# Off-by-one attention and slotted soft MoE: one exponential for both heads of a pair, on a hand-numbered ring of PSUM banks

## The chip, the cores and the metric

The kernel runs on one core of one Trainium2 chip (trn2). The metric is the time of one execution in microseconds on the device. Five engines with queues of their own take part: TensorE (PE; its weight loads are shown as PEld), VectorE (DVE), ScalarE (ACT), GpSimd (POOL), which also issues most of the DMAs, and SyncE (SP), which issues the others. The sums of TensorE stand in PSUM, in eight banks of 2 KB for each of 128 partitions.

## The reference

```python
# q, k, v: (8, 12, 448, 64)
scores = scale * np.matmul(q, k.transpose(0, 1, 3, 2))
m = np.max(scores, axis=-1, keepdims=True)
e = np.exp(scores - m)
attn = e / (np.sum(e, axis=-1, keepdims=True) + np.exp(-m) + 1e-09)
x = np.matmul(attn, v)                 # heads side by side: (3584, 768)

logits = x @ phi                       # phi: (768, 32), 8 experts of 4 slots
d = softmax of logits over the 3584 tokens
slot_input = d.T @ x                   # (32, 768)
for e in range(8):                     # on the 4 slots of expert e
    slot_out[e] = np.maximum(slot_input[e] @ w1[e], 0) @ w2[e]    # 768 -> 1024 -> 768
c = softmax of logits over the 32 slots
out = c @ slot_out                     # (3584, 768), float32
```

The first softmax has one more term, exp(-m), in its denominator. Maxima and exponentials of the scores are what the change is about.

## The kernel before

**Work.** The 96 pairs of batch and head are taken two heads at a time: NPAIR = 48 pairs, six (PB) to a batch, three (NP) to a group of loads. The two heads of a pair (hl = 0, 1) lie in the lower and upper 64 partitions. 448 tokens make three chunks of 128 and a half chunk of 64 (i = 3), in which both heads share the partitions. The program's order is kept as written on each engine (`manual_schedule`), so a queue waits when its next instruction waits.

**Slots.** The main loop has a slot s for each pair, with two halves y = 0 and 1. The parts of a slot:

- `T(n)`: 28 transposes of q and k of pair n (L262) into one bank, and one copy to SBUF, by ScalarE (L269) or VectorE (L271). In slot s it is pair s + 4.
- `A(n, i)`: the scores with queries on partitions (L290, or L307 for the half chunk) into a bank of `psA` (three banks) and their row maxima by VectorE (L291, L309). `runs` is the list of these, and each chunk of the loop takes the next one. They run one to two pairs ahead.
- `W2(n)`: turns the maxima of pair n (L316); VectorE copies them (mT, L318).
- `Bk(n, i)`: the scores with keys on partitions (L354, L383), from which `lower` takes the maximum by four more products (L337), and their exponentials by ScalarE (L358, L388). With `mix=True` the products of the next `A` are laced in: a0 of head 0, scores of head 1, scores of head 0, the four lowering products, the exponentials, a1 of head 1.
- `AV(n, i, qs)`: products of the exponentials with v and a column of ones (L422), into the one bank of `psV`; the ones give the denominators.
- `N1(n)`: copies that bank to `ubuf` (L435). `EC(g)`: exp(-m) of a group (L323). `N2(n)`: denominator by one VectorE instruction (L450), its reciprocal (L451), and by GpSimd three products that write x (L463), and two small instructions for the half chunk (L471, L472).
- `PX(n)`: turns x of pair n by four products (L493) into one bank, which ScalarE copies (L499). In slot s it is pair s - 2.
- `V(g)` (L394 to L397) and `slot_loads`: GpSimd's placing of v and its DMA issues, one group ahead. `P(b)` is the soft-MoE work of a batch (logits L527, their turn and maxima, exponentials, the sums of L615); its steps are spread over slots by `post`.

Before the change a slot goes so on TensorE: chunk 0, chunk 1 | twenty products of `AV`, W2 | chunk 2, half chunk, T, twelve products of `AV`, PX.

**Banks.** `psA` has three banks, `psV` one, and `psB` four that are taken in turn, one at a time, by the scores of `Bk` (two for a chunk, one for the half chunk), by T and by PX: nine takings a slot. A taking waits until the reader of the one four before is done.

After the loop the eight experts (L825, L845) and the output (L888) follow; they take the last 45 us or so, and the change leaves them as they are.

Of the kernel before, what the change touches and what calls it, by code (L numbers as in the profile page):

```python
# [24 lines left out]
HG = 6  # L25
NP = 3
# [5 lines left out]
def kernel(  # L32
# [123 lines left out]
    with ExitStack() as at:  # L156
# [9 lines left out]
        ubuf = pu.tile([128, 2, 7 * W65], F32, name="ubuf")  # L166
# [32 lines left out]
        def ones_in(t, eng):  # L199

            eng.memset(t, 0.0)
            eng.memset(t[:, :, 0:3, D:W65], 1.0)
            eng.memset(t[0:64, 0:HG:2, 3, D:W65], 1.0)
            eng.memset(t[64:128, 1:HG:2, 3, D:W65], 1.0)
# [3 lines left out]
        for hl in range(2):  # L208
            nc.vector.memset(halfm[64 - 64 * hl:128 - 64 * hl, hl:hl + 1], 1.0)
# [24 lines left out]
        def kcol(hl, tok):  # L234
            if hl == 0:
                return 384 if tok == 0 else (tok - 1) * 128 if tok < 4 else (tok - 4) * 128 + 64
            return tok * 128 if tok < 3 else (tok - 3) * 128 + 64 if tok < 6 else 384

        def qcol(hl, i):

            if i < 2:
                return slice(i * 128, i * 128 + 128)
            if i == 2:
                return slice(320, S) if hl == 0 else slice(256, 384)
            return slice(256, 320) if hl == 0 else slice(384, S)

        def T(n):
            g, pl = divmod(n, NP)
            first = n < 7
            ps = psB.tile([128, 2, S], BF16, tag="b", name="ps_t")  # L250

            k0 = [psB.tile([128, 2, S], BF16, tag="b", name="ps_k") for _ in range(2)] if n == 0 else None
# [11 lines left out]
            if n == 0:  # L264
                nc.scalar.copy(t[:, 0, :], ps[:, 0, :])
                nc.vector.tensor_copy(t[:, 1, 0:256], k0[0][:, 0, 0:256])
                nc.vector.tensor_copy(t[:, 1, 256:S], k0[1][:, 0, 256:S])
            elif first or n % 6 in (1, 3):
                nc.scalar.copy(t, ps)  # L269
            else:  # L270
                nc.vector.tensor_copy(t, ps)  # L271
            qkT[n] = t

        def mpos(i, hl=0):
            return 3 if i == 3 else i if hl else (5, 6, 4)[i]
# [5 lines left out]
        def A(n, i, steps=False):  # L283
# [18 lines left out]
            else:  # L302
                ps = psA.tile([128, 512], F32, tag="a", name="ps_a")

                for hl in range(2):
                    r = slice(64 * hl, 64 * hl + 64)
                    nc.tensor.matmul(ps[64 - 64 * hl:128 - 64 * hl, 0:S], t[r, 0, qcol(hl, 3)], t[r, 1, :],  # L307
# [12 lines left out]
        def EC(g):  # L320
            ec[g] = psm.tile([128, NP, 7], F32, tag="ec", name="ec", bufs=3)
            z = g % 2 * NP
            nc.scalar.activation(ec[g], mxr[:, z:z + NP, 0:7], AF.Exp, scale=-scale)  # L323
            if g == NG - 1:
                e, t = ec[g][:, NP - 1, :], psm.tile([128, 7], F32, name="ec_last", bufs=1)
                for o, i in ((slice(1, 6, 2), slice(0, 3)), (slice(0, 4, 2), slice(5, 7)), (slice(4, 5), slice(4, 5)),
                             (slice(6, 7), slice(3, 4))):
                    nc.gpsimd.tensor_copy(t[:, o], e[:, i])
                ec["last"] = t

        def lower(outs, n, m):

            for z in range(2):
                for hl, o in outs.items():
                    c = (5, 3) if hl == 0 else (0, 2)
                    src = slice(0, 256) if z == 0 else slice(64, 256) if hl == 0 else slice(0, 192)
                    nc.tensor.matmul(o[:, 256 * z:min(256 * z + 256, S)], sel[rs[hl], c[z]:c[z] + 1].to_broadcast([64, m]),  # L337
# [3 lines left out]
        def Bk(n, i, c=0, mix=False):  # L341

            t = qkT[n]
            if i < 3 and mix and runs and runs[0][1] < 3:
# [5 lines left out]
                pss = {}  # L350

                def score(hl):
                    pss[hl] = pb_("ps_b")
                    nc.tensor.matmul(pss[hl][:, 0:S], t[rs[hl], 1, cols], t[rs[hl], 0, :], start=True, stop=False,  # L354
                                     skip_group_check=True)

                def expo(hl):
                    nc.scalar.activation(e[:, hl, :], pss[hl][:, 0:S], AF.Exp, scale=scale)  # L358
                    eT[n, i, hl] = e[:, hl, :]
# [4 lines left out]
                lower({hl: pss[hl][:, 0:S] for hl in (1, 0)}, n, 128)  # L364
                expo(1)
                expo(0)
                a1()
                return
            if i < 3:
                pss = [pb_("ps_b") for _ in range(2)]  # L370
                outs = [p[:, 0:S] for p in pss]
# [4 lines left out]
            else:  # L376
                pss = [pb_("ps_b")]
                outs = [pss[0][r, 0:S] for r in rs]
# [8 lines left out]
            for p, e in zip(pss, es):  # L387
                nc.scalar.activation(e, p[:, 0:S], AF.Exp, scale=scale)  # L388
# [3 lines left out]
        def V(g):  # L392
            t, s = vp[g % 2], nat["v", g]
            nc.gpsimd.tensor_copy(t[:, 0:HG:2, 0:3, 0:D], s[:, 0:HG:2, 1:4, :])  # L394
            nc.gpsimd.tensor_copy(t[:, 1:HG:2, 0:3, 0:D], s[:, 1:HG:2, 0:3, :])
            nc.gpsimd.tensor_copy(t[0:64, 0:HG:2, 3, 0:D], s[0:64, 0:HG:2, 0, :])
            nc.gpsimd.tensor_copy(t[64:128, 1:HG:2, 3, 0:D], s[64:128, 1:HG:2, 3, :])  # L397
# [9 lines left out]
        def AV(n, i, qs):  # L407
# [6 lines left out]
            for u in qs:  # L414
                for hl in range(2):
                    if u < 3:
                        c0 = (2 * u + hl if n == NPAIR - 1 else mpos(u, hl)) * W65
                        o, qc = a[:, c0:c0 + W65], qcol(hl, u)
                    else:
                        t, z = (av_half["ps"], 0) if n == NPAIR - 1 else (a, 3 * W65)  # L420
                        o, qc = t[64 - 64 * hl:128 - 64 * hl, z:z + W65], qcol(hl, 3)
# [7 lines left out]
        def N1(n):  # L429
            src = av[n][:, 0:7 * W65].rearrange("p (s c) -> p s c", c=W65)  # L430
            if n == NPAIR - 1:
                us[n] = src
                return
            u = ubuf[:, n % 2, :].rearrange("p (s c) -> p s c", c=W65)
            (nc.scalar.copy if on_pool(n) else nc.vector.tensor_copy)(u, src)  # L435
            us[n] = u

        def N2(n):
            g, pl = divmod(n, NP)
            b, pb = divmod(n, PB)  # L440
            u = us[n]
            eng = nc.gpsimd if on_pool(n) else nc.vector
            rec = psm.tile([128, 7], F32, tag="rec", name="rec", bufs=3)
            e = ec[g][:, pl, :] if n < NPAIR - 1 else ec["last"]
            if n == NPAIR - 1:
                nc.vector.scalar_tensor_tensor(rec[:, 6:7], av_half["ps"][:, D:W65], 1e-9, e[:, 6:7],
                                               op0=ALU.add, op1=ALU.add)
                nc.vector.scalar_tensor_tensor(rec[:, 0:6], u[:, 0:6, D], 1e-9, e[:, 0:6], op0=ALU.add, op1=ALU.add)
            else:
# [5 lines left out]
            if n == NPAIR - 1:  # L455
                eng.tensor_mul(
                    x[:, 0:3, c:c + 128].rearrange("p i (h d) -> p i h d", h=2),
                    u[:, 0:6, 0:D].rearrange("p (i h) d -> p i h d", h=2),
                    rec[:, 0:6].rearrange("p (i h) -> p i h", h=2).unsqueeze(3).to_broadcast([128, 3, 2, D]))
            else:  # L460
# [4 lines left out]
            if n == NPAIR - 1:  # L465

                for h in range(2):
                    r = slice(64 - 64 * h, 128 - 64 * h)
                    nc.scalar.mul(x[r, 3, c + 64 * h:c + 64 * h + 64], av_half["ps"][r, 0:D], rec[r, 6:7])
                return  # L470
# [3 lines left out]
                u[:, 3, 0:D].unsqueeze(1).to_broadcast([128, 2, D]),  # L474
# [200 lines left out]
        runs = [(n, i) for n in range(NPAIR) for i in (0, 1, 3, 2)]  # L675
# [50 lines left out]
        for s in range(NPAIR + 1):  # L726
            for y in range(2):
                hs = 2 * s + y
                mix = len(runs) > 1 and runs[0][1] == 2 - y
                if mix:  # L730
                    Bk(s, 2 * y, mix=True)
                    Bk(s, 2 * y + 1, y, mix=True)
                else:
                    As(1)
                if mix:
                    pass
                elif s < NPAIR:
                    Bk(s, 2 * y)
                    side = int(y == 1 and len(runs) > 0 and runs[0][1] == 3)
                    Bk(s, 2 * y + 1, side)  # L740
                    As(1 - side)
                else:
                    As(1)
# [4 lines left out]
                else:  # L748
                    if s < NPAIR - 4:
                        T(s + 4 if s else 3)  # L750
                    if s < NPAIR:
                        for i in (0, 1):
                            AV(s, i, range(3))
# [241 lines left out]
```

## Time and profile before

| what | value |
|---|---|
| median of 3 runs | 304.77 us (303.82 to 565.14) |
| the profiled execution | 303.48 us, its span 301.4 us |
| mean granted TensorE clock | 0.952 |
| busy: PE, DVE, ACT, POOL | 274.6, 259.4, 245.1, 197.4 us |
| row maxima (L291, VectorE) | 276 of 613 ns |
| exponentials of a chunk (L358, ScalarE) | 276 of 566 ns |
| copies of turned q,k (L269 ScalarE; L271 VectorE) | 20 of 923 ns; 27 of 612 ns |
| copies of turned x (L499, ScalarE) | 47 of 607 ns |
| products for x (L463, GpSimd) | 135, of 505, 395 and 289 ns by size |

Busy times are unions: neighbouring instructions on an engine overlap a little, so the mean length of an instruction is more than its share of a full engine. The busy time of PE counts modelled ends of its pipelined products. In the answers shown below a line of instructions has the start in us from the start of the span, the time until the last of the group ends, engine, line, operation, what it writes and reads, and how many.

### The profile page before, as it was taken

What the parts mean: (1) busy time and instruction counts of PE and PEld (TensorE: products, weight loads), DVE (VectorE), ACT (ScalarE), POOL (GpSimd) and SP (SyncE); (2) the same over time, 40 slices, a digit from 0 to 9 for tenths busy, and PEclk for the clock granted to TensorE, in tenths of its full rate; (3) what the DMA queues carried; (4) which work ended last, traced back from release to release, by engine and by line L of the source; (5) the groups of instructions that cost most, each with busy time, mean ns of one, the idle gap of its engine ahead of it and who ended that gap; (6) DMA issues with size and microseconds to landing.
All of it is one profiled execution on the core that took longest, in us unless ns stands there. A gap on an engine that the chain in (4) does not pass through costs nothing.

```text
span 301.4 us, 13421 instructions
## 1 busy us (share of the span) xinstructions
PE 274.6 (91%) x5682; PEld 190.3 (63%) x5682; DVE 259.4 (86%) x626; ACT 245.1 (81%) x524; POOL 197.4 (65%) x433
## 2 busy tenths in 40 slices
PE   5899999999999999999999999999999999997820
PEld 3476767776766677767776777677767666662100
DVE  5989999999999999999999999999999996537840
ACT  3489999899889989998999899988998978337730
POOL 8767696878688959795979597959892763000000
PEclk9889999999999999999999999999999999998555
DMA  8999399999999999999999999999999699907997
GB/s 138 193 196 200 55 127 213 166 207 148 211 144 194 140 210 153 203 144 211 150 203 151 206 144 206 159 194 164 209 174 210 100 226 239 345 20 290 409 446 320
DMA packets 47275, 58.93 MB, mean 196 GB/s; under 512 B 2800, under 2 KB 40176, under 8 KB 46960
## 3 DMA queue, kind: packets, MB, share of 16 engines
q0 software_dynamic: 40432, 42.29, 87.8%
q1 hardware_dynamic: 6784, 15.80, 13.7%
q8 instruction: 44, 0.72, 0.9%
q14 instruction: 15, 0.12, 0.1%
HBM read 89.36 MB, written 15.34 MB: 347 GB/s over the span
## 4 chain that ended last, share of the span: by engine, by line
PE 58%; ACT 16%; DVE 16%; issue 5%; DMA 1%; DVEq 0%; ACTq 0%
PE ps_av L422 12%; PE ps_a L290 10%; DVE mxr L291 8%; PE ps_b L337 8%; PE ps_b L354 5%; ACT W L269 4%; PE ps_b L383 4%; PE ps_t L262 4%; ACT W L388 3%; ACT W L358 3%; ACT W L499 3%; PE ps_o L888 3%; PE ps_x L493 2%; PE ps_s L615 2%; PE ps_h L825 2%
## 5 line engine op out<-in xcount | busy, mean ns | idle before, releaser
L291 DVE TENSOR_REDUCE mxr<-ps_a 128x1 bf16<-128x448 f32 x276 | 153.7, 613 | 5.2 <-PE ps_a L290 5.0
L358 ACT ACTIVATE W<-ps_b 128x448 bf16<-128x448 f32 x276 | 131.8, 566 | 9.8 <-PE ps_a L290 5.4
L337 PE MATMUL ps_b<-mT,sel 64*128 64x192 bf16 (+3 forms) x768 | 94.3, 258 | 0.0
L290 PE MATMUL ps_a<-W 64*128 64x448 bf16 x276 | 90.2, 354 | 2.3 <-DVE mxr L291 1.9
L354 PE MATMUL ps_b<-W 64*128 64x448 bf16 x276 | 78.2, 354 | 2.6 <-ACT W L269 0.5
L463 POOL TENSOR_TENSOR W<-ubuf,rec 128x192 bf16<-128x192 f32 x135 | 50.0, 396 | 39.4 <-ACT W L499 25.3
L422 PE MATMUL ps_av<-W 128*128 128x65 bf16 (+1 forms) x1536 | 64.7, 196 | 0.6 <-issue 0.5
L422 PEld LDWEIGHTS <-W 128*128 128x128 bf16 (+1 forms) x1536 | 50.1, 100 | 21.5 <-issue 17.2
L337 PEld LDWEIGHTS <-sel 64*128 64x128 bf16 (+1 forms) x768 | 48.3, 98 | 22.5 <-issue 8.9
L499 ACT CAST W<-ps_x 128x512 bf16<-128x512 f32 x47 | 28.5, 607 | 10.8 <-PE ps_x L493 10.5
L388 ACT ACTIVATE W<-ps_b 128x448 bf16<-128x448 f32 x60 | 32.5, 562 | 1.6 <-PE ps_b L337 1.5
L290 PEld LDWEIGHTS <-W 64*128 64x128 bf16 x276 | 25.9, 94 | 11.6 <-issue 0.4
L262 PE MATMUL ps_t<-ident,W 64*64 64x64 bf16 x1330 | 29.8, 195 | 1.4 <-ACT W L213 1.4
L262 PEld LDWEIGHTS <-W 64*64 64x64 bf16 x1344 | 28.3, 112 | 3.6 <-issue 2.0
L309 DVE TENSOR_REDUCE mxr<-ps_a 128x1 bf16<-128x448 f32 x48 | 29.5, 615 | 0.1
L435 ACT COPY ubuf<-ps_av 128x455 f32<-128x455 f32 x45 | 26.1, 579 | 1.2 <-PE ps_av L422 0.6
L111 POOL DMA_DIRECT2D W<-in_moe_w_dram x30 | 22.6, 754 | 5.2 <-PE ps_b L337 4.2
L269 ACT COPY W<-ps_t 128x896 bf16<-128x896 bf16 x20 | 18.5, 923 | 3.8 <-PE ps_t L262 3.8
L383 PE MATMUL ps_b<-W 64*64 64x448 bf16 (+1 forms) x108 | 21.2, 375 | 0.1
L472 POOL TENSOR_TENSOR W<-ubuf,rec 128x128 bf16<-128x128 f32 x45 | 18.0, 400 | 3.7
L354 PEld LDWEIGHTS <-W 64*128 64x128 bf16 x276 | 18.2, 94 | 3.3 <-issue 1.9
L493 PE MATMUL ps_x<-ident,W 128*128 128x128 bf16 x192 | 18.7, 219 | 0.2
(146 smaller groups left out, 394.5 us busy)
## 6 DMA issues: line engine op xcount, KB each, us to landing
W<-in_moe_w_dram POOLq DMA_DIRECT2D x22, 768.0 KB, 9.6
W<-in_v_dram POOLq DMA_DIRECT2D x32, 192.0 KB, 4.9
out_dram<-W SPq DMA_DIRECT2D x2, 2688.0 KB, 9.3
W<-in_q_dram POOLq DMA_DIRECT2D x15, 336.0 KB, 4.9
W<-in_k_dram POOLq DMA_DIRECT2D x15, 336.0 KB, 6.6
stage<-in_moe_w_dram POOLq DMA_DIRECT2D x4, 768.0 KB, 10.1
W<-stage SPq DMA_DIRECT2D x5, 576.0 KB, 6.0
W<-in_moe_w_dram POOLq DMA_DIRECT2D x4, 576.0 KB, 8.1
```

The source lines that it names most:

```text
L262: nc.tensor.transpose(o, src[r, pl, tok * D:(tok + 1) * D], ident[r, r])
L269: nc.scalar.copy(t, ps)
L290: nc.tensor.matmul(ps[:, 0:S], t[r, 0, qcol(hl, i)], t[r, 1, :], start=True, stop=True)
L291: nc.vector.reduce_max(mcol(n, i, hl), ps[:, 0:S], axis=AX.X)
L337: nc.tensor.matmul(o[:, 256 * z:min(256 * z + 256, S)], sel[rs[hl], c[z]:c[z] + 1].to_broadcast([64, m]), mT[n][rs[hl], src], start=False, ...
L354: nc.tensor.matmul(pss[hl][:, 0:S], t[rs[hl], 1, cols], t[rs[hl], 0, :], start=True, stop=False, skip_group_check=True)
L358: nc.scalar.activation(e[:, hl, :], pss[hl][:, 0:S], AF.Exp, scale=scale)
L383: nc.tensor.matmul(outs[hl], t[rs[hl], 1, cols], t[rs[hl], 0, :], start=True, stop=False, skip_group_check=True)
L388: nc.scalar.activation(e, p[:, 0:S], AF.Exp, scale=scale)
L422: nc.tensor.matmul(o, eT[n, i, hl][:, qc], vp[g % 2][:, 2 * pl + hl, i, 0:W65], start=(i == 0 and u == 0 and hl == 0) or (u == 3 and i == ...
L463: eng.tensor_mul(x[:, i0:i1, c + 64 * h:c + 64 * h + 64], u[:, r, 0:D], rec[:, r].unsqueeze(2).to_broadcast([128, i1 - i0, D]))
L499: nc.scalar.copy(xT(b, pb), pss[0])
```

## The change

1. **Ring.** `psB` becomes one tile of four banks. `pb_(nm, n)` hands out the next bank, or for n = 2 the next two that begin at an even number; a bank left over is passed by.
2. **Exponentials.** Both heads of a chunk have their scores in two neighbouring banks, and one ScalarE instruction takes the exponentials of both (896 columns).
3. **Order.** In the second half of a slot the half chunk comes first, then T, then chunk 2; `runs` is in the order 0, 3, 1, 2. So a slot goes: chunk 0, chunk 1 | `AV`, W2 | half chunk, T, chunk 2, `AV`, PX.
4. **Turned copies.** From pair 7 on the copy of T goes to ScalarE for two pairs of three (before for one of three), and stands behind the exponential of chunk 2 (`late_copy`).
5. **Denominators.** `EC` adds 1e-9 on GpSimd; a new step `N1a` adds exp(-m) and the sums on GpSimd, behind N1 (in a group's last slot behind EC). VectorE keeps the reciprocal.
6. **x.** The two heads change places in the half chunk (`kcol`, `qcol`, `mpos`, `lower`, `V`), so that `ubuf` holds them as two rows of four and one GpSimd product of 3 x 2 x 64 writes what three wrote. The last pair needs no GpSimd copies of its exp(-m) any more.

```diff
-        psB = pool("psB", 4, space=PSUM)
+        psB = pool("psB", 1, space=PSUM)
-        pb_ = lambda nm: psB.tile([128, 512], F32, tag="b", name=nm)
+        ring = psB.tile([128, 4, 512], F32, name="ring")
+        at_bank = [0]
+        def pb_(nm="", n=1):
+            z = -(-at_bank[0] // n) * n % 4
+            at_bank[0] = (z + n) % 4
+            return ring[:, z, :] if n == 1 else ring[:, z:z + n, :]
+        pt_ = lambda: pb_().bitcast(BF16)[:, 0:2 * S].rearrange("p (a s) -> p a s", a=2)
...
         def T(n):
-            ps = psB.tile([128, 2, S], BF16, tag="b", name="ps_t")
+            ps = pt_()
...
-            elif first or n % 6 in (1, 3):
+            elif first:
                 nc.scalar.copy(t, ps)
+            elif n % 3 != 2:
+                late_copy.append((t, ps))
             else:
                 nc.vector.tensor_copy(t, ps)
...
         def EC(g):
-            ec[g] = psm.tile([128, NP, 7], F32, tag="ec", name="ec", bufs=3)
+            ec[g] = psm.tile([128, NP, 8], F32, tag="ec", name="ec", bufs=3)
-            nc.scalar.activation(ec[g], mxr[:, z:z + NP, 0:7], AF.Exp, scale=-scale)
-            if g == NG - 1:
...
+            nc.scalar.activation(ec[g][:, :, 0:7], mxr[:, z:z + NP, 0:7], AF.Exp, scale=-scale)
+            nc.gpsimd.tensor_scalar(ec[g][:, :, 0:7], ec[g][:, :, 0:7], 1e-9, None, op0=ALU.add)
...
         def Bk(n, i, c=0, mix=False):
...
-                    pss[hl] = pb_("ps_b")
+                ps = pb_("ps_b", 2)
...
-                expo(1)
-                expo(0)
+                nc.scalar.activation(e, ps[:, :, 0:S], AF.Exp, scale=scale)
+                for hl in range(2):
+                    eT[n, i, hl] = e[:, hl, :]
                 a1()
...
+        def N1a(n):
+            rec = psm.tile([128, 8], F32, tag="rec", name="rec", bufs=3)
+            u = ubuf[:, n % 2, :].rearrange("p (s c) -> p s c", c=W65)
+            nc.gpsimd.tensor_add(rec[:, 0:7], u[:, 0:7, D], ec[n // NP][:, n % NP, 0:7])
+            us[n] = rec
...
         def N2(n):
-                nc.vector.scalar_tensor_tensor(rec, u[:, :, D], 1e-9, e, op0=ALU.add, op1=ALU.add)
-            nc.vector.reciprocal(rec, rec)
-                for i0, i1, z, h in ((0, 3, 0, 1), (0, 2, 5, 0), (2, 3, 4, 0)):
-                    r = slice(z, z + i1 - i0)
-                    eng.tensor_mul(x[:, i0:i1, c + 64 * h:c + 64 * h + 64], u[:, r, 0:D],
-                                   rec[:, r].unsqueeze(2).to_broadcast([128, i1 - i0, D]))
+            rec, eng = us[n], nc.gpsimd if on_pool(n) else nc.vector
+            nc.vector.reciprocal(rec[:, 0:7], rec[:, 0:7])
+            u = ubuf[:, n % 2, :].rearrange("p (h i c) -> p h i c", h=2, i=4)
+            eng.tensor_mul(xs, u[:, :, 0:3, 0:D].rearrange("p h i d -> p i h d"),
+                           rec.rearrange("p (h i) -> p i h", h=2)[:, 0:3, :].unsqueeze(3).to_broadcast([128, 3, 2, D]))
...
-        runs = [(n, i) for n in range(NPAIR) for i in (0, 1, 3, 2)]
+        runs = [(n, i) for n in range(NPAIR) for i in (0, 3, 1, 2)]
...
+                order = (0, 1) if y == 0 else (3, 2)
+                if s < NPAIR:
+                    Bk(s, order[0], int(y and len(runs) > 0), mix=True)
+                if y and s < NPAIR - 4:
+                    T(s + 4 if s else 3)
+                if s < NPAIR:
+                    Bk(s, order[1], mix=True)
+                while late_copy:
+                    nc.scalar.copy(*late_copy.pop())
...
                         N1(s - 1)
+                        if s - 1 < NPAIR - 1 and s % 3 != 1:
+                            N1a(s - 1)
                         if s % 3 == 1:
                             EC((s - 1) // 3)
+                            N1a(s - 1)
```

More of the change, by code (lines that the diff above doesn't have):

```diff
@@ L249, in T @@
             first = n < 7
-            ps = psB.tile([128, 2, S], BF16, tag="b", name="ps_t")
-            k0 = [psB.tile([128, 2, S], BF16, tag="b", name="ps_k") for _ in range(2)] if n == 0 else None
+            ps = pt_()
+            k0 = [pt_() for _ in range(2)] if n == 0 else None
             for a in range(2):
@@ L272, in T @@
             qkT[n] = t
+        late_copy = []
         def mpos(i, hl=0):
-            return 3 if i == 3 else i if hl else (5, 6, 4)[i]
+            return 3 if i == 3 else 4 * hl + i
         def mcol(n, i, hl=0):
@@ L334, in lower @@
                 for hl, o in outs.items():
-                    c = (5, 3) if hl == 0 else (0, 2)
-                    src = slice(0, 256) if z == 0 else slice(64, 256) if hl == 0 else slice(0, 192)
-                    nc.tensor.matmul(o[:, 256 * z:min(256 * z + 256, S)], sel[rs[hl], c[z]:c[z] + 1].to_broadcast([64, m]),
+                    row = (0, 2) if hl == 0 else (3, 5)
+                    src, dst = (slice(0, 256), slice(0, 192), slice(64, 256))[2 * hl * (1 - z) + (1 - hl) * z], \
+                        ((slice(0, 256), slice(256, S)), (slice(0, 192), slice(192, S)))[hl][z]
+                    nc.tensor.matmul(o[:, dst], sel[rs[hl], row[z]:row[z] + 1].to_broadcast([64, m]),
                                      mT[n][rs[hl], src], start=False, stop=True, skip_group_check=True)
@@ L363, in Bk @@
                 score(0)
-                lower({hl: pss[hl][:, 0:S] for hl in (1, 0)}, n, 128)
-                expo(1)
-                expo(0)
+                lower({hl: ps[:, hl, 0:S] for hl in (1, 0)}, n, 128)
+                nc.scalar.activation(e, ps[:, :, 0:S], AF.Exp, scale=scale)
+                for hl in range(2):
+                    eT[n, i, hl] = e[:, hl, :]
                 a1()
@@ L369, in Bk @@
             if i < 3:
-                pss = [pb_("ps_b") for _ in range(2)]
-                outs = [p[:, 0:S] for p in pss]
+                ps = pb_("ps_b", 2)
+                outs = [ps[:, hl, 0:S] for hl in range(2)]
                 cols = slice(i * 128, (i + 1) * 128)
@@ L376, in Bk @@
             else:
-                pss = [pb_("ps_b")]
-                outs = [pss[0][r, 0:S] for r in rs]
+                ps, e = pb_("ps_b"), e1_t
+                outs = [ps[r, 0:S] for r in rs[::-1]]
                 cols = slice(384, 448)
@@ L386, in Bk @@
             lower(dict(enumerate(outs)), n, m)
-            for p, e in zip(pss, es):
-                nc.scalar.activation(e, p[:, 0:S], AF.Exp, scale=scale)
+            nc.scalar.activation(e, ps[:, :, 0:S] if i < 3 else ps[:, 0:S], AF.Exp, scale=scale)
             for hl in range(2):
@@ L440, in N2 @@
             b, pb = divmod(n, PB)
[L441 to L449, printed above, removed]
-                nc.vector.scalar_tensor_tensor(rec, u[:, :, D], 1e-9, e, op0=ALU.add, op1=ALU.add)
@@ L465, in N2 @@
[L465 to L470, printed above, removed]
+            xs = x[:, 0:3, c:c + 128].rearrange("p i (h d) -> p i h d", h=2)
+            if n == NPAIR - 1:
+                rec = psm.tile([128, 8], F32, tag="rec", name="rec", bufs=3)
+                e = ec[g][:, pl, :].rearrange("p (h i) -> p h i", h=2)
+                u = av[n][:, 0:6 * W65].rearrange("p (h i c) -> p h i c", h=2, i=3)
+                r6 = rec[:, 0:6].rearrange("p (h i) -> p h i", h=2)
+                nc.vector.tensor_add(rec[:, 6:7], av_half["ps"][:, D:W65], ec[g][:, pl, 3:4])
+                nc.vector.tensor_add(r6, u[:, :, :, D], e[:, :, 0:3])
+                nc.vector.reciprocal(rec[:, 0:7], rec[:, 0:7])
+                nc.vector.tensor_mul(xs, u[:, :, :, 0:D].rearrange("p h i d -> p i h d"),
+                                     r6.rearrange("p h i -> p i h").unsqueeze(3).to_broadcast([128, 3, 2, D]))
+                for h in range(2):
+                    nc.scalar.mul(x[rs[h], 3, c + 64 * h:c + 64 * h + 64], av_half["ps"][rs[h], 0:D], rec[rs[h], 6:7])
+                return
@@ L747 @@
                             AV(s - 1, i, range(3))
[L748 to L753, printed above, removed]
+                elif s < NPAIR:
+                    for i in (0, 1):
+                        AV(s, i, range(3))
                 for f in post.get(hs, ()):
```

73 lines of the change are left out of this document (20 added, 53 removed).

## The prediction

> **What bounds the kernel now.** I read the page first, for the share of each engine, then stretches of the main loop, then the instructions of one slot in order of time, engine by engine. The page:
>
> ```profile
> span 301.4 us, 13421 instructions
> PE 274.6 (91%) x5682; PEld 190.3 (63%) x5682; DVE 259.4 (86%) x626; ACT 245.1 (81%) x524; POOL 197.4 (65%) x433
> ...
> L291 DVE TENSOR_REDUCE mxr<-ps_a 128x1 bf16<-128x448 f32 x276 | 153.7, 613 | 5.2 <-PE ps_a L290 5.0
> L358 ACT ACTIVATE W<-ps_b 128x448 bf16<-128x448 f32 x276 | 131.8, 566 | 9.8 <-PE ps_a L290 5.4
> ...
> L499 ACT CAST W<-ps_x 128x512 bf16<-128x512 f32 x47 | 28.5, 607 | 10.8 <-PE ps_x L493 10.5
> ...
> L269 ACT COPY W<-ps_t 128x896 bf16<-128x896 bf16 x20 | 18.5, 923 | 3.8 <-PE ps_t L262 3.8
> ```
>
> Three engines are nearly full, so no share decides alone. The stretches do: six slots (one period of the loop), then a slot whose turned q,k copy (L269) is ScalarE's, then one where it is VectorE's. Columns: busy us of PE, PEld, DVE, ACT, POOL, granted clock, DMA share, GB/s.
>
> ```profile
> 95.12:125.45 30.33, 29.81 (x663) 21.79 (x661) 29.03 (x71) 27.71 (x63) 24.68 (x54) 1.00 1.08 175
> 99.82:104.66 4.84, 4.70 (x108) 3.32 (x106) 4.54 (x12) 4.84 (x12) 4.65 (x11) 1.00 0.98 127
> 34.79:39.37 4.58, 4.58 (x110) 3.36 (x108) 4.52 (x11) 4.45 (x12) 4.25 (x10) 1.00 0.38 43
> ```
>
> A slot with ScalarE's copy takes 4.84 us, with ScalarE busy in all of it; one with VectorE's copy 4.58, with VectorE busy 4.52. With the per-batch soft-MoE work the period is 30.33 us, 5.06 a slot. The instructions of TensorE in the 4.58 us slot (start, length):
>
> ```profile
> 34.99 0.36 PE L290 MATMUL ps_a<-W 64*128 64x448 bf16 x1
> 35.49 0.24 PE L337 MATMUL ps_b<-mT,sel 64*128 64x192 bf16 x1
> 35.67 0.38 PE L383 MATMUL ps_b<-W 64*64 64x448 bf16 x2
> 36.08 0.60 PE L262 MATMUL ps_t<-ident,W 64*64 64x64 bf16 x28
> 36.61 0.54 PE L422 MATMUL ps_av<-W 128*128 128x65 bf16 x12
> 36.99 0.39 PE L493 MATMUL ps_x<-ident,W 128*128 128x128 bf16 x4
> 37.30 0.36 PE L290 MATMUL ps_a<-W 64*128 64x448 bf16 x1
> 37.88 0.35 PE L290 MATMUL ps_a<-W 64*128 64x448 bf16 x1
> ```
>
> From start to start: chunk 2 takes 0.68 us (0.50 to its last lowering product, L337), the half chunk 0.41, the turns 0.53, the twelve products with v 0.38, PX 0.31, chunk 0 0.58. By the rest of that answer chunk 1 takes 0.86, of which some 0.18 waits for a VectorE maximum (chunk 2, unhindered, takes 0.68), the twenty products with v 0.62, W2 0.21. Their sum without that wait, 0.68 + 0.41 + 0.53 + 0.38 + 0.31 + 0.58 + 0.68 + 0.62 + 0.21 = 4.40, is what TensorE needs for a slot.
>
> And ScalarE in the 4.84 us slot, the wait that matters here:
>
> ```profile
> 101.66 0.55 ACT L388 ACTIVATE W<-ps_b 128x448 bf16<-128x448 f32 x1
> 102.08 0.93 ACT L269 COPY W<-ps_t 128x896 bf16<-128x896 bf16 x1
> 102.87 0.63 ACT L499 CAST W<-ps_x 128x512 bf16<-128x512 f32 x1
> ```
>
> One step to the next is 0.42, 0.79 and 0.47 us, each 0.13 to 0.16 under its own length, since neighbours overlap. In the chain TensorE's next scores (L354) start at 103.55, 0.05 after that last copy ends: chunk 1 takes the banks of T and PX, and waits for both copies.
>
> **The change, part by part.** *Exponentials.* Two of 448 columns (step 0.42 each) become one of 896. The trace has none; the nearest row is the copy of 896 columns, L269: 0.92 long, step 0.79. Bounds: 0.85, along the line through L358 (448, 0.566) and L499 (512, 0.607), and 1.13, two of L358 with nothing saved. I take 0.92. That saves ScalarE 0.05 x 3 a slot, 7 us in all, but it holds both banks until the whole has ended.
>
> *Copies of turned q,k.* From pair 7 on there are 41. Before, n % 6 in (1, 3) gives ScalarE 14; now n % 3 != 2 gives it 27. So 13 x 0.79 = 10 us go to ScalarE, and 13 x 0.53 = 7 leave VectorE.
>
> *Denominators.* The add (L450, 0.163) leaves VectorE: with its gap 0.18 x 45 = 8 us. VectorE then needs 7 maxima x 0.53 + mT 0.20 + reciprocal 0.12 = 4.0 to 4.1 a slot, 4.6 with a copy; it no longer bounds a slot without one. GpSimd gets an add per pair and one per group, near L471 (0.286). The reciprocal now waits for GpSimd's queue. Once in three slots V (L394 to L397) and two loads of v stand there, until 128.57 in the slot where the reciprocal (L451) ran at 128.51; with the two adds behind them it would run at 129.15, 0.65 late. Behind it on VectorE stand the next maxima, for which TensorE waits with three banks of psA. I charge nothing, since in that stretch TensorE waits longer for ScalarE (below); without that cover it is at most 16 x 0.65 = 10 us.
>
> *x in one product.* GpSimd's three, 505 + 395 + 289 ns, become one of 384 elements: 0.83 by the line through these three sizes, at most 1.19 as before. GpSimd is 65% busy and PX comes a slot later: nothing on the path.
>
> *Ring and order: here the time is decided.* A pair of banks must start at an even number. With chunk 0 on A and chunk 1 on B, the half chunk takes A's first bank, T its second, chunk 2 takes B, PX A's first; the next chunk 0 finds an odd number, skips that bank and lands on B again. So chunk 0 always wants **the pair that chunk 2 has just left**, and chunk 1 that of T and PX. Before, four single banks in turn put the half chunk, T and PX between a bank's uses. From the start of chunk 2's last lowering product (0):
>
> - TensorE starts the products with v at 0.18, PX at 0.56, chunk 0 at 0.87, and wants its scores' banks at once.
> - The exponential starts at 0.29 (that product 0.24, hand-over 0.05) and ends at 1.21; the scores start at 1.26. **Wait: 0.39.**
> - Chunk 1 wants its scores at 1.26 + 0.58 = 1.84. ScalarE's next step is at 0.29 + 0.79 = 1.08. With the turned copy on VectorE, PX's copy runs from there and ends at 1.71: no wait. With it on ScalarE (`late_copy` stands ahead of PX), that copy takes 1.08 to 1.87, PX's ends at 2.49, the scores start at 2.54. **Wait: 0.70 more.**
>
> Nothing is left to fill these waits: the half chunk and the turns, 0.94 us that stood between chunk 2 and the products with v, are now ahead of chunk 2. ScalarE has its own gap of that size ahead of chunk 2's exponential, so neither catches up. VectorE's slot becomes 4.40 + 0.39 = 4.79, ScalarE's 4.40 + 0.39 + 0.70 = 5.49. Six slots hold two and four of them: 31.5. Of the soft-MoE work the logits (24 products, 0.60 in the chain), a broadcast and its weight load (0.25) add 0.85; the 28 products of L615 (0.69) fall into the waits. Sum 32.4 against 30.33: 2.05 a period, or 6.8 x 2.05 = **14 us over the 41 slots**. Slots 44 to 46, without turns, take 15.9 now by the starts of W2 and lose some 1 us by VectorE's relief; the drain gains some 0.3 by one more hop through GpSimd. The four small GpSimd copies of the last group fall away off the path.
>
> The profiled execution took 303.5 us (span 301.4 and 2.1 around it); 303.5 + 13.3 = 316.8. The median of the three runs is 1.3 higher, so I put 317. The exponential's bounds shift both waits alike: at 0.85 a slot takes 0.07 less, 314; at 1.13 it takes 0.21 more, 326.
>
> **The rivals.** *The ring does not bind, and VectorE's relief shows.* Then a period is bound by TensorE: 6 x 4.40 and 1.7 of soft-MoE products, 28.1 against 30.33 (1.7: the 0.60, 0.69 and 0.25 above and small ones), so 15 us less: 288. For it: VectorE is busy 29.03 of 30.33 today, and loses 15 us in all. Against it: the two waits. It decides as soon as they average under some 0.35 us a slot (my sum has 0.39 + 0.70 x 2/3 = 0.86), so chunk 2's exponential would have to end before TensorE is through v and PX. The DMA queues, a share of 1.08 in the period, would take part of it: 288 to 298.
>
> *Relief and waits cancel*, with the copy wait half its size: 41 x 0.35 x 2/3 = 9.6 off, near 306.
>
> *GpSimd's queue bounds the reciprocal*, with ring waits elsewhere: 317 + 16 x 0.5 = 325.
>
> *The granted clock falls.* After a 3.41 us stretch with TensorE 73% busy (9.86 to 13.27: 2.48) the trace shows one of 3.42 at 0.50. In the changed slot 1.09 us of waiting can lie in one such stretch: 68%. Half clock for one stretch costs some 1.7 us of TensorE's work, less the 1.0 of waiting that it fills: 0.7 x 27 = 19, so 336. Against it: that fall came once, in the ramp, and no stretch of the loop shows what 68% would do.
>
> The Trainium skill, "TensorE: Matmul & The Clock Gate", section "A second HAM failure mode: psum-queue depth-cycling", says of another kernel that cycling through PSUM banks left TensorE so many micro-idles that its clock swung between half and full. That speaks against this change; the row at 13.27 shows such a fall once, in the ramp, and the loop of before, at 98% busy, none. By that rule the sum would be 336, without it 317.
>
> **How the numbers follow.** Forecast (both waits) 0.58, GpSimd's queue 0.06, clock 0.08: slower 0.72. Cancelling: 0.08. Ring hidden: 0.20, since the schedule rests on start times of one slot. 2% is 6 us, about what a measurement of this kernel tells from no change. The likeliest case alone spans 314 to 326; the range for 8 in 10 reaches to 296, leaving out the lower half of the hidden case, and to 332, leaving out most of the clock case.
>
> **What would show it.** TensorE idle ahead of the chunk scores (L354's successor), released by the merged exponential in every slot and by PX's copy in two of three; ScalarE's exponentials as some 144 rows of 128x896 near 0.92; VectorE's busy share down to some 78%; slots of some 5.5 and 4.8 us. Wrong if the slots are under 4.8 throughout, if these waits are under 10 us in total, or if the merged row is far from 0.92.

## Result and profile after

The changed kernel takes 565.43 us (median of 4 runs, 561.4 to 577.98); the kernel before took 303.24 to 304.77 in three runs beside it. The ratio is 1.856 with a 95% interval of 1.834 to 1.878; it leaves out one run of each kernel that was longer than its others, the 577.98 here and the 565.14 in the table above for the kernel before; what made that one so long is not on record. The forecast said slower, but 317 us with a range of 296 to 332: the measured time lies far outside it. The profiled execution took 562.25 us.

From the page of the changed kernel, the lines that answer to those shown of before:

```profile
span 560.5 us, 13131 instructions
PE 416.8 (74%) x5682; PEld 240.7 (43%) x5682; DVE 269.1 (48%) x562; ACT 265.7 (47%) x393; POOL 199.4 (36%) x402
...
PEclk9996755775896755865767557575559566888965
...
L302 DVE TENSOR_REDUCE mxr<-ps_a 128x1 bf16<-128x448 f32 x278 | 168.2, 624 | 181.3 <-PE ps_a L301 181.3
L367 ACT ACTIVATE W<-ring 128x896 bf16<-128x896 f32 x139 | 127.5, 917 | 175.8 <-PE ring L344 122.0
```

VectorE, ScalarE and GpSimd are busy about as long as before (269.1, 265.7 and 199.4 us, where it was 259.4, 245.1 and 197.4), in a span nearly twice as long. VectorE and ScalarE stand and wait for TensorE (181.3 and 175.8 us of idle time ahead of these two groups alone), and TensorE runs at a mean granted clock of 0.700, where it was 0.952. The merged exponential takes 917 ns, as forecast.

Where the time went, by the starts of W2 and of the experts: from TensorE's first product to the first W2 9.6 us (before 8.8), from the first to the last W2 483.6 (237.2), from there to the experts 18.8 (12.7), from the experts to the end of the last instruction 36.2 (30.5). (Some 1 us ahead of these stretches and some 11 us of output transfers behind them are the same in both.) So the loop lost 246 us and what follows it 12.

Single slots and a longer stretch of the loop (columns as before: busy us of PE, PEld, DVE, ACT, POOL, granted clock, DMA share, GB/s):

```profile
153.04:162.11 9.07, 6.26 (x134) 4.00 (x130) 5.29 (x11) 4.85 (x9) 4.41 (x9) 1.00 0.49 55
202.89:214.28 11.39, 9.59 (x136) 5.85 (x134) 5.08 (x10) 5.21 (x7) 5.71 (x11) 0.50 0.47 71
267.12:330.31 63.19, 48.16 (x663) 28.22 (x661) 30.51 (x62) 30.63 (x45) 25.00 (x49) 0.66 0.58 86
```

There are two losses, one on top of the other. At full clock a slot takes 9.07 us instead of 4.6 to 5.4, with no engine near full. Where the clock is at 0.50 it takes 11.39. A slot at full clock, TensorE's instructions on the ring in order of time (start, length; in brackets the idle time before and who ended it):

```profile
151.72 0.37 PE L360 MATMUL ring<-W 64*128 64x448 bf16 x2 [0.82 <-ACT W L367]
...
153.34 0.38 PE L386 MATMUL ring<-W 64*64 64x448 bf16 x2
...
154.60 0.63 PE L269 MATMUL ring<-ident,W 64*64 64x64 bf16 x28 [0.69 <-ACT W L390]
...
156.01 0.36 PE L360 MATMUL ring<-W 64*128 64x448 bf16 x2 [0.49 <-DVE W L280]
...
157.57 0.38 PE L490 MATMUL ring<-ident,W 128*128 128x128 bf16 x4 [0.36 <-ACT W L367]
...
158.63 0.37 PE L360 MATMUL ring<-W 64*128 64x448 bf16 x2 [0.38 <-ACT W L496]
...
160.19 0.36 PE L360 MATMUL ring<-W 64*128 64x448 bf16 x2 [0.82 <-ACT W L367]
```

Read who releases whom. The turns (L269, at 154.60) are written into the second bank of pair A, and the exponential that releases them (L390) reads the first. Chunk 2's scores (156.01) go to pair B and are released by the copy (L280) that reads the turns' bank in A. PX (157.57) goes to A and is released by chunk 2's exponential on B; chunk 1 (151.72 and 160.19) and chunk 0 lie on different pairs too. **Every write into the ring waits for the reader just before it, whichever bank that reads.** The half chunk (153.34) waits for chunk 1's exponential too; it has no bracket because the products with v and W2 fill that wait: it starts 0.05 after that exponential's end (153.29).

So the ring works like a single buffer: write, read, write, read. From chunk 1 of one slot to that of the next the steps are 1.62 (half chunk), 1.26 (turns), 1.41 (chunk 2), 1.56 (PX), 1.06 (chunk 0), 1.56 (chunk 1), together 8.47 us. (The slot of 9.07 also holds the 24 products of the logits, behind chunk 1.) Each of the two 1.56 is the scores with their lowering products, 0.59, the exponential, 0.92, and 0.05 to hand over.

### The profile page after: what moved, and what is told of

The parts are those of the page before. It is cut to its first block, busy times and chain, and to the rows that moved or that the text cites. A ratio compares the mean times of both kernels' runs of the same rounds, so it can differ in the third digit from the quotient of the medians.

```text
span 560.5 us, 13131 instructions
## 1 busy us (share of the span) xinstructions
PE 416.8 (74%) x5682; PEld 240.7 (43%) x5682; DVE 269.1 (48%) x562; ACT 265.7 (47%) x393; POOL 199.4 (36%) x402
## 4 chain that ended last, share of the span: by engine, by line
PE 60%; ACT 30%; issue 3%; DVE 3%; DMA 0%; DVEq 0%; ACTq 0%
ACT W L367 14%; PE ring L344 11%; PE ps_av L424 10%; PE ring L360 10%; PE ring L269 7%; PE ps_a L301 6%; ACT W L390 5%; ACT W L496 5%; PE ring L386 4%; PE ring L490 4%; ACT W L734 4%; DVE W L280 2%; PE ps_m L327 1%; PE ps_o L879 1%; PE ring L836 1%
## 5 line engine op out<-in xcount | busy, mean ns | idle before, releaser
L302 DVE TENSOR_REDUCE mxr<-ps_a 128x1 bf16<-128x448 f32 x278 | 168.2, 624 | 181.3 <-PE ps_a L301 181.3
L367 ACT ACTIVATE W<-ring 128x896 bf16<-128x896 f32 x139 | 127.5, 917 | 175.8 <-PE ring L344 122.0
L301 PE MATMUL ps_a<-W 64*128 64x448 bf16 x278 | 114.8, 488 | 0.0
L360 PE MATMUL ring<-W 64*128 64x448 bf16 x278 | 74.8, 467 | 51.6 <-ACT W L367 31.9
L344 PE MATMUL ring<-mT,sel 64*128 64x192 bf16 (+3 forms) x768 | 106.8, 342 | 0.0
L465 POOL TENSOR_TENSOR W<-ubuf,rec 128x384 bf16<-128x384 f32 x45 | 37.7, 838 | 144.4 <-DVE rec L463 144.4
L269 PE MATMUL ring<-ident,W 64*64 64x64 bf16 x1344 | 39.0, 218 | 32.0 <-ACT W L390 30.7
L269 PEld LDWEIGHTS <-W 64*64 64x64 bf16 x1344 | 39.3, 133 | 49.7 <-issue 48.2
L390 ACT ACTIVATE W<-ring 128x448 bf16<-128x448 f32 (+1 forms) x53 | 30.7, 579 | 27.3 <-PE ring L344 26.4
L496 ACT CAST W<-ring 128x512 bf16<-128x512 f32 x47 | 27.5, 586 | 27.8 <-PE ring L490 27.7
L386 PE MATMUL ring<-W 64*64 64x448 bf16 (+1 forms) x106 | 27.7, 516 | 5.1 <-ACT W L390 2.4
L318 PE MATMUL ps_a<-W 64*64 64x448 bf16 x96 | 25.9, 536 | 0.4 <-DVE mxr L312 0.4
```

Of the source, the lines that this page charges most:

```text
L269: nc.tensor.transpose(o, src[r, pl, tok * D:(tok + 1) * D], ident[r, r])
L301: nc.tensor.matmul(ps[:, 0:S], t[r, 0, qcol(hl, i)], t[r, 1, :], start=True, stop=True)
L302: nc.vector.reduce_max(mcol(n, i, hl), ps[:, 0:S], axis=AX.X)
L344: nc.tensor.matmul(o[:, dst], sel[rs[hl], row[z]:row[z] + 1].to_broadcast([64, m]), mT[n][rs[hl], src], start=False, stop=True, skip_group ...
L360: nc.tensor.matmul(ps[:, hl, 0:S], t[rs[hl], 1, cols], t[rs[hl], 0, :], start=True, stop=False, skip_group_check=True)
L367: nc.scalar.activation(e, ps[:, :, 0:S], AF.Exp, scale=scale)
```

## The experiments

The kernel before took 303.6 to 303.8 us beside all of them.

**One tile, and nothing else of the change.** Before's code with its four banks as one tile, still handed out one at a time, in the old order, with two exponentials.

```diff
-        psB = pool("psB", 4, space=PSUM)
+        psB = pool("psB", 1, space=PSUM)
+        ring = psB.tile([128, 4, 512], F32, name="ring")
...
-        pb_ = lambda nm: psB.tile([128, 512], F32, tag="b", name=nm)
+        def pb_(nm=""):
+            z = at_bank[0]
+            at_bank[0] = (z + 1) % 4
+            return ring[:, z, :]
```

> The kernel before with one thing changed: its four banks of psB are one tile of four banks, handed out one at a time in the same turn. Theory A (one tile, one wait: every write into the ring waits for the last read of the ring, whichever bank it was): chunk 1 waits for chunk 0's exponentials, the half chunk for chunk 2's, T for the half chunk's, PX for T's copy, chunk 0 for PX's copy; some 1.2 + 1.2 + 0.8 + 0.7 + 0.7 = 4.6 us a slot on 4.4, so 9 us a slot and 480 us at full clock, up to 570 where the clock falls. Theory B (waits by bank, and the rest of the loss is the fallen clock and the merged exponential): 304, within 2%.

Measured: 581.1 us in a single execution, clock 0.694, a little over the 570 that was expected at most. This alone makes the whole loss, though the numbering and the order are the old ones. The longest wait of TensorE (us in all, times, longest) is that of the half chunk's scores (L391) for chunk 2's exponentials (L366), which read other banks:

```profile
PE ring L391 <- ACT W L366: 49.8, 46, 1.1
```

Neither the merged exponential nor the order nor the pairs of banks is needed for it.

**The change, with the ring's waits by bank.** Every write into the ring is told to wait for the last reader of its own bank only; the order on each engine stays.

```diff
+        def wrote(ins, z):
+            own = last_read[z]
+            tc.declare_no_dep(ins.ins, group="ring", keep=[own] if own is not None else [], reason="other banks")
+            if own is not None:
+                tc.add_manual_dep(ins.ins, own.name, ..., reason="own bank")
+        def read(ins, *zs):
+            tc.add_to_no_dep_group("ring", ins.ins)
+            for z in zs:
+                last_read[z] = ins.ins
```

> The changed kernel whole, with the waits of the ring drawn by bank: each write waits for the last read of its own bank and for no other. Theory A: the two waits of the prediction are what is left, 0.39 in every slot and 0.70 more where ScalarE copies the turned q,k, so 317 (310 to 332), TensorE at full clock or nearly. Theory B: little changes, over 450.

Measured: 322.25 us, ratio 1.062 [1.060, 1.064], clock 0.962. Some 243 of the 262 us are gone, with the banks, the exponential and the order of the change. So it was the waits that the program was given that held the ring up, and not the banks. The waits that the forecast had worked out are what is left of the ring's. Its TensorE and then its ScalarE in a slot with ScalarE's copy of the turned q,k:

```profile
139.32 0.36 PE L320 MATMUL ps_a<-W 64*128 64x448 bf16 x1
139.70 0.36 PE L380 MATMUL ring<-W 64*128 64x448 bf16 x2
...
140.09 0.35 PE L320 MATMUL ps_a<-W 64*128 64x448 bf16 x2
140.50 0.85 PE L380 MATMUL ring<-W 64*128 64x448 bf16 x2
140.99 0.46 PE L363 MATMUL ring<-mT,sel 64*128 64x192 bf16 x3
```

```profile
138.73 0.92 ACT L387 ACTIVATE W<-ring 128x896 bf16<-128x896 f32 x1 [0.32 <-PE ps_a L320]
139.54 0.90 ACT L757 COPY W<-ring 128x896 bf16<-128x896 bf16 x1
140.33 0.60 ACT L518 CAST W<-ring 128x512 bf16<-128x512 f32 x1
```

Chunk 0's maxima product runs at 139.32, its scores only at 139.70, 0.05 after the exponential's end at 139.65: 0.38 (forecast 0.39). Chunk 1's maxima product runs at 140.09, its first scores at 140.50, after the copy of the turned q,k (until 140.44): 0.41. The second head's scores wait for PX's copy (until 140.93), so the lowering products start 0.49 after the first scores, where chunk 0 has 0.20: 0.29 more. Together 0.70, as forecast.

One thing in this slot was not in the forecast. Here are the half chunk's scores, its first lowering products, the first turns and chunk 2's first product:

```profile
137.19 0.38 PE L407 MATMUL ring<-W 64*64 64x448 bf16 x2
137.41 0.27 PE L363 MATMUL ring<-mT,sel 64*64 64x256 bf16 x2
137.41 0.26 PE L286 MATMUL ring<-ident,W 64*64 64x64 bf16 x6
137.95 0.36 PE L320 MATMUL ps_a<-W 64*128 64x448 bf16 x1
```

The turns start together with the lowering products, 0.22 after the scores; in the kernel before they start 0.41 after them, in nearly every slot. Half chunk and turns take 0.76 us together, where the sum of before has 0.94.

**What the fallen clock costs.** The changed kernel, with ten small products on TensorE, whose result nothing uses, behind chunk 0, behind the half chunk, ahead of PX and behind it.

```diff
+        def fill(k):
+            ps = psA.tile([128, 512], F32, tag="a", name="ps_f")
+            for _ in range(k):
+                nc.tensor.matmul(ps[:, 0:128], ident, ident, start=True, stop=True)
```

> The changed kernel with idle products on TensorE added in the places where it waits for the ring: ten of 128x128 by 128 columns behind chunk 0, the half chunk, and ahead of and behind PX (some 2.2 us of extra TensorE work a slot, nothing of it is used). Theory A (the waits leave TensorE so idle that its clock falls, and that makes slots of 9.0 us into 11.4): the clock stays near 1.00 in the loop and the slots near 9.05, so about 490 to 505 us in spite of the added work. Theory B (the fallen clock is not due to the waits, or costs nothing of its own): 565 or more.

Measured: 483.95 us in a single execution, a little under the 490 to 505 expected. From its page, TensorE's busy time and its granted clock:

```profile
PE 424.5 (88%) x7602; PEld 301.8 (63%) x7602; DVE 266.0 (55%) x562; ACT 263.6 (55%) x393; POOL 199.1 (41%) x402
...
PEclk9999999999999999999999999999999999999955
```

With 1920 products more the kernel is 81 us faster, since the clock stays at full speed in the loop. The waits stay: its slots take 8.5 to 9.1 us. So, if the added products shorten no wait, at least 79 of the loop's 246 us come from the clock (483.6 from the first to the last W2, 404.5 here), and at most 167 from the waits; the added products' own cost is inside the 167.

**The change's order, copies, denominators and x product, on four single banks** (two exponentials a chunk, the copy by ScalarE issued at once).

```diff
-        psB = pool("psB", 1, space=PSUM)
+        psB = pool("psB", 4, space=PSUM)
...
-                late_copy.append((t, ps))
+                nc.scalar.copy(t, ps)
...
-                nc.scalar.activation(e, ps[:, :, 0:S], AF.Exp, scale=scale)
+                for hl in (1, 0):
+                    nc.scalar.activation(e[:, hl, :], ps[hl][:, 0:S], AF.Exp, scale=scale)
```

> The changed kernel with four single banks in turn as before and so two exponentials of 448 for a chunk, and with ScalarE's copy of the turned q,k issued with T and not behind chunk 2's exponentials; order, split of copies, denominators and x as changed. Theory A: no wait of the ring is left and VectorE is relieved; a slot with ScalarE's copy is bound by ScalarE (7 x 0.42 + 0.79 + 0.47 + 0.42 = 4.65, some 4.75), one without by TensorE (4.5), so a period of 28.9 against 30.3 and 294 us. Theory B (order or GpSimd's part cost something of their own): 305 to 320.

Measured: 313.25 us, 1.034 [1.027, 1.041]. This expectation was missed by 19 us. The slots with VectorE's copy, once in three, average 6.25 and 6.03 us against 5.38 and 4.71 before; the others are near or under those of before. Those long slots are the ones in which GpSimd has V and the loads of v.

**Only the denominators on GpSimd and the single x product**, with the exchange of heads that it needs, on before's banks and order.

```diff
+        def N1a(n):
+            nc.gpsimd.tensor_add(rec[:, 0:7], u[:, 0:7, D], ec[n // NP][:, n % NP, 0:7])
...
-                nc.vector.scalar_tensor_tensor(rec, u[:, :, D], 1e-9, e, op0=ALU.add, op1=ALU.add)
             nc.vector.reciprocal(rec[:, 0:7], rec[:, 0:7])
```

> The kernel before in banks, exponentials, order and split of copies, with only the denominators and the one product for x as changed. Theory A: VectorE is 0.18 us a slot lighter, which shows in the four slots of six that it bounds: 4.9 us less, 299. Theory B (GpSimd's queue holds up the reciprocal once in three slots, 0.3 to 0.65 us each): 304 to 312.

Measured: 310.85 us, 1.025 [1.022, 1.029]. GpSimd's queue, then the reciprocal on VectorE:

```profile
129.61 0.73 POOL L181 DMA_DIRECT2D W<-in_v_dram  x1
130.34 0.67 POOL L182 DMA_DIRECT2D W<-in_v_dram  x1
131.06 0.66 POOL L590 TENSOR_TENSOR acc<-acc,corr 128x224 f32<-128x224 f32 x1
131.81 0.27 POOL L327 TENSOR_SCALAR ec<-ec 128x21 f32<-128x21 f32 x1
132.17 0.21 POOL L434 TENSOR_TENSOR rec<-ubuf,ec 128x7 f32<-128x7 f32 x1
132.41 0.20 DVE L457 RECIPROCAL rec<-rec 128x7 f32<-128x7 f32 x1 [1.04 <-POOL rec L434]
```

The adds stand behind V's copies, two DMA issues and a soft-MoE addition; VectorE waits 1.04 us here, 15.0 in 16 such waits of the run, and its maxima are queued behind the reciprocal. TensorE waits 11.9 us for maxima in this run (L293 for L294), where it was 1.9 before.

**The same, with each group's first pair added on VectorE again**, the one that falls behind V and the loads.

> The kernel of e4 with the denominator of each group's first pair added on VectorE as before; that is the pair whose add stands in GpSimd's queue behind V and two loads. The other two of three stay on GpSimd. Theory A: the waits of the reciprocal (15.0 us, 16 times in e4) go, VectorE's relief is left in two slots of three: 298 to 301. Theory B (small adds on GpSimd cost in every slot): 304 to 311.

Measured: 302.07 us, 0.996 [0.994, 0.998]. One add of three on VectorE takes back nearly 9 us; what is left of this part, with the exchange of heads, gains some 0.4%. So it is the place in the queue, not GpSimd's work, that cost the time. In this kernel and in the one before it, on before's banks and order, the turns start 0.22 us after the half chunk's scores in every slot, as in the run with waits by bank. So that gain of 0.19 us a slot on TensorE comes with part 6 and not with the ring or the order. In the kernel before, the lowering products of the half chunk read and write the same half of the partitions, as the turns do; after the exchange they read one half and write the other. All nine kernels that have the exchange and are free of the ring's waits show the 0.22 in most of their slots, but the exchange was not tried by itself.

**Waits by bank, with the denominators on VectorE**, and reads of different banks by ScalarE and VectorE not ordered among themselves either (in the run with waits by bank alone, ScalarE's exponential waited 13 times, 9.8 us in all, for VectorE's copy of another bank).

> The kernel of e2 (waits by bank) with reads of different banks by ScalarE and VectorE not ordered against each other either, and with the denominators added on VectorE as before. Theory A (the slots with V are long for GpSimd's queue, ahead of the reciprocal, and for chunk 2's exponential behind VectorE's copy): those two slots of six fall from 6.15 and 5.53 us to some 5.45 and 4.85, a period of 31.0, so 309 us, still slower than before by the two waits of the prediction. Theory B (GpSimd's queue is not it): 320.

Measured: 315.37 us, 1.037 [1.035, 1.040], 7 us under the run with waits by bank alone; the expectation was 6 too low. The two long slots of six go from 6.15 and 5.53 to 5.41 and 5.13; the run changes two things at once, and how much each gave was not tried. A period takes 31.0, as expected: what was missed lies behind the loop. There the one tile still costs its time, here ahead of the experts' first products (which write one bank of the ring while ScalarE reads another):

```profile
269.13 1.48 PE L849 MATMUL ring<-W,ubuf 128*32 128x512 bf16 x24 [1.52 <-ACT ubuf L854]
```

From the experts to the end of the last instruction this kernel takes 36.4 us, before 30.5: the waits by bank were written for the loop's writes alone.

**On top of that, ScalarE's copy of the turned q,k at once instead of behind chunk 2's exponential**, and then also **PX in a bank of `psA`**.

> The kernel of e6 (waits by bank, denominators on VectorE, merged exponentials) with ScalarE's copy of the turned q,k issued with T and not behind chunk 2's exponential. By the prediction's own schedule chunk 1's wait (0.70) goes, and chunk 0's (0.39) grows by some 0.25, as chunk 2's exponential comes later: ScalarE's slots 5.11 to some 4.9, 6 us less than e6 in all: 309. If chunk 1 did not wait for that copy: 315 as e6.

> The kernel of e10 with PX's bank taken from psA and not from the ring, so that chunk 0 no longer lands on the pair that chunk 2 has just left. By the prediction's schedule chunk 0's wait goes (its pair was last read by the copy of T, long done), and psA makes the next maxima wait some 0.3: ScalarE's slots 4.7, the loop some 8 us shorter than in e10, 301 in all with what the one tile costs after the loop (some 6 us). If chunk 0's wait was not due to the pair: no gain on e10.

Measured: 312.76 us, 1.031 [1.029, 1.033], and 307.0, 1.012 [1.009, 1.015]. The early copy gains 2.6 of an expected 6, PX's own bank 5.8 of an expected 8. Both expectations were 4 to 6 us too low, and the misses lie in the loop, since the stretch after it is the same in all three (36.4 us again). With the early copy ScalarE's slots take 4.96 to 5.14 us (expected 4.9). With PX's own bank chunk 0's scores follow its maxima product at once (132.15 and 132.16), but the next maxima product waits up to 0.5 for PX's copy (8.6 us in 22 such waits; expected 0.3 each), and most slots take 4.87 (expected 4.7). In the loop the last one takes 235.7 us, before 237.2.

**The order, the copies and the x product on four single banks, with the denominators on VectorE.**

```diff
 (against the run on four single banks above)
-            nc.gpsimd.tensor_add(rec[:, 0:7], u[:, 0:7, D], ec[n // NP][:, n % NP, 0:7])
...
+                nc.vector.scalar_tensor_tensor(rec[:, 0:7], ..., 1e-9, ec[g][:, pl, 0:7], op0=ALU.add, op1=ALU.add)
```

> The kernel of e3 (order of the slot, two of three turned copies on ScalarE and issued at once, x in one product; single banks, two exponentials) with the denominators on VectorE as before. Theory A: the slots of e3 without GpSimd's wait, 4.74 + 5.0 + 5.4 + 4.85 + 4.78 + 4.75 = 29.5 a period against 30.3: 298, faster than before. Theory B (order and split cost by themselves): 304 to 310.

Measured: 299.46 us, 0.986 [0.984, 0.988]: 1.4% faster than the kernel before, and the fastest here. Which of its parts gives the 1.4% was not tried; the exchange of heads is one of them. With the adds of two pairs of three on GpSimd again it takes 300.37, 0.988 [0.985, 0.992], no gain:

> The kernel of e8 with the adds of each group's second and third pair on GpSimd, as in e7, where they do not stand behind V. Theory A: VectorE 0.18 us lighter in two slots of three, but ScalarE or TensorE bound these (4.75 to 4.80), so little: 298 to 300, no more than 1 us from e8. Theory B (GpSimd's queue bites again): 301 to 304.

## Why the prediction was wrong

- **The step that failed** is "Ring and order: here the time is decided". It let each write wait for the reader of its own bank. "Before, four single banks in turn" is right for before, where the four are four buffers. The diff makes them one tile, and in the profile after a write into that tile waits for the last reader of any part of it. One tile alone gives 581 us; the same kernel with waits by bank 322. Had the sum gone by tile, it would have had the write, read, write chain of the slot above, 8.47 us, some 400 over the loop's 47 steps from W2 to W2, and so by this estimate a time near 465 before any fall of the clock. That the four banks might not be four buffers was never drawn up as a rival; this was that case: the ring has four banks and one bank's worth of freedom. That the change would be slower was not luck, since it is so with waits by bank too (1.062), but nine tenths of the loss have a cause that the forecast did not hold.
- **The granted clock** was the right mechanism with a chance of 0.08 and a wrong size. I priced 0.7 us for one fallen stretch a slot, on waits of 1.09 us. TensorE stands idle for 2.81 us of the slot of 9.07, more than twice as long, and a slot goes from 9.07 to 11.39 at half clock. "Against it: that fall came once, in the ramp" said nothing on a loop that is no longer 98% busy. The Trainium skill, "TensorE: Matmul & The Clock Gate", section "A second HAM failure mode: psum-queue depth-cycling", says of another kernel that the many short idle times of such cycling make the clock swing between half and full. This case's trace agrees: 0.700 on average with the waits, 0.975 with the same waits filled, 0.962 without most of them.
- **The two waits as such** (0.39 and 0.70) are in the run with waits by bank, at 0.38 and 0.70. The slot around them was too long by 0.38: 5.11 us, not 5.49. The turns run together with the half chunk's lowering products (both together 0.76, not 0.94), which comes with part 6, for which nothing was counted on TensorE. And of the held-up chunk 0 the two heads' scores start together (139.70), so that its 0.58 becomes 0.39.
- **"I charge nothing"** for GpSimd's queue was wrong. The cover named for it, TensorE waiting longer for ScalarE in that stretch, is not there in the slots with VectorE's copy. The denominators and the x product on before's banks cost 7 us, and 9 come back with one add of three. The bound of 10 that I gave was about right.
- **The time after the loop** was charged nothing and rose by 12 us. The experts take their banks from the same ring, so the change does not leave them as they are.
- **Right:** the merged exponential 0.92 (917 ns measured), the x product 0.83 (840), GpSimd's add under 0.286 (204). They decide nothing here. With waits by bank, the errors in the slots, in GpSimd's queue and after the loop nearly cancel, 322 against 317, and that nearness is luck.

What stays open: the best version with one tile and merged exponentials takes 235.7 us in the loop, that with single banks and two exponentials 232.7. Whether these 3 us come from the merged exponential, which holds both banks longer, or from PX's bank in `psA` was not tried by itself. Nor was a ring of two tiles of two banks each, in which the merged exponential would keep a second buffer.

## To carry to other kernels

When buffers that were taken one by one become slices of one tile, ask first what the waits are drawn by. If it is by tile, the number of buffers is one, whatever the numbering says; look in the profile for a write released by the reader of another slice. And ahead of moving a small instruction to a less busy engine, read what stands in that engine's queue at that moment: a 0.2 us add behind copies and two DMA issues cost more than the work it took off VectorE.

## What was not expected of the hardware

- More work made the kernel faster: with 1920 products more on TensorE, 484 us instead of 565, since the granted clock stayed at 0.975 instead of 0.700.
- Waits of 0.4 to 0.8 us each are enough to bring the clock down, and not at once: the slot at 153.04, with TensorE busy 6.26 of 9.07 us (69%), still had full clock, while the six slots from 267.12 had 0.66 on average (busy 76%, as the same work counts for longer at the lower clock). What sets the moment was not measured.
- The turns can run together with the half chunk's lowering products: 0.76 us for half chunk and turns, 0.18 less than the sum of their steps in the kernel before. Other banks are not enough for it, since the kernel before had these too; it is seen only in kernels with the heads exchanged in the half chunk.
